# Reordering the first two stages of a retention and feed-forward kernel: two blocks of tokens per quarter of the weights, weight conversion ahead of a chunk that loads late

## The chip, the core and the metric

The kernel runs on one core of a Trainium2 (trn2) chip. The metric is the device time of one execution in microseconds; the figure quoted for a kernel is the median of its executions. The engines are called as the profile calls them: PE is TensorE (matrix products, and transposes as products with an identity), PEld its weight load, DVE is VectorE, ACT is ScalarE, POOL is GpSimd, SP starts the transfers.

## The reference

```python
# q, k, v: (8, 8, 576, 64) float32
scores = scale * q @ k^T                    # per batch and head
ret    = (scores * Dmat[head]) @ v          # Dmat: causal mask with a decay
x      = ret.transpose(0, 2, 1, 3).reshape(4608, 512)
a, b   = x @ w1, x @ w2                     # w1, w2: (512, 1024) float64
h      = (a * b) @ w3                       # w3: (1024, 1024) float64
out    = (h @ w_out).astype(float32)        # w_out: (1024, 512) float64
```

The weights arrive as float64, that is as pairs of 32-bit words, and the chip itself turns them into float32. They are cut into 40 blocks of 128 x 512: 16 for w1 and w2 (four in each quarter), 8 for w_out, 16 for w3.

## The kernel before

The eight batches are taken in four pairs. A pair is five chunks of the sequence (`NC`) for the attention, and three blocks of 192 tokens per batch (`NB`) for the products with w1 and w2. Those are done by quarters of the weights (`NQ` = 4), each by Strassen's scheme. A *unit* is one block of tokens times one quarter: seven products of eight matrix instructions. It needs three things: the quarter converted, the sums S1 to S4 of the weights (DVE), and the sums T of the tokens (POOL).

```python
def scale(g, nm):                       # decay into q or v of chunk g
    nc.gpsimd.tensor_tensor(out=t[:sz], in0=t[:sz], in1=..., op=ALU.mult)

def front(g):                           # 16 transposes of k and q, copied out by ACT
    ...
    nc.scalar.copy(dst[:, b, :, :sz], tp[:, :, :sz])

def score(g):                           # scores, then the mask product on DVE
    ...
    nc.vector.tensor_mul(pm[:sz, b, j, :, :sz], sc[j][:sz, :, :sz], mask...)

# state(g): running k^T v, 32 instructions; pv(g): the attention's output, copied by ACT into xT

def begin_block():                      # three DVE steps and two exponent operations on ACT
    vec.tensor_scalar(out=e, in0=hi, ...); yield
    vec.tensor_scalar(out=m, in0=hi, ...); yield
    vec.scalar_tensor_tensor(m.bitcast(F32), in0=lo.bitcast(U32), ...)
    nc.scalar.activation(e, e, relu, bias=lim[:, 0:1], scale=-1.0)
    nc.scalar.activation(e, e, relu, bias=lim[:, 1:2], scale=-2.0 ** 23)
    yield

def end_block():                        # two more DVE steps, then the next load
    vec.scalar_tensor_tensor(e, in0=hi, ..., in1=e, ...); yield
    vec.scalar_tensor_tensor(out, in0=m, ..., in1=e, ...)      # into wA
    load_block()
    if key[0] == "w12" and key[2:] == (1, 1):
        strassen_weights(key[1])        # S1, S2, S3, S4: four DVE sums into wS and wA
    yield

# convert(n): n of these steps. convert_up_to(n): steps until block n is converted.

def strassen_tokens(i, n):              # four subtractions on POOL, three T buffers
    T = [ffn.tile([P, 2, TB], F32, tag="T", name="T", bufs=4) for _ in range(3)]
    ...

def up(i, n, fp, conv=0):               # the unit: block n of pair i, quarter fp
    convert_up_to(4 * (fp + 1))
    if ("B", i, n) not in live:
        strassen_tokens(i, n)
    ...
    c = ffn.tile([P, 4, 2, TB], F32, tag="c", name="c")        # two buffers
    p1 = product(None, "A11", "B11")
    nc.scalar.copy(c[:, 0], p1)
    plus(product(None, "S2", "T2"), 1, 0)   # plus: DVE sum, then convert(conv)
    ...                                     # five more products: four DVE sums, one ACT copy
    nc.vector.tensor_mul(ab[:, 4 * fp:4 * fp + 4, :], c[:, :, 0, :], c[:, :, 1, :])
    convert(conv)

# ---- main program, first part ----
for g in range(NC):
    if g + 1 < NC:
        if g + 2 < NC:
            load(g + 2, "kq")
        scale(g + 1, "q"); front(g + 1); scale(g + 1, "v")
    pv(g)
    if g + 2 < NC:
        load(g + 2, "v")
    if g == 1:
        strassen_tokens(0, 0)
    if g + 1 < NC:
        state(g + 1)
        if g == 1:
            convert_up_to(KD)           # KD = 4: quarter 0
        else:
            convert(10)
        score(g + 1)
    if 0 < g < NC - 1:
        up(0, 0, g - 1, conv=1)         # block 0 alone, one quarter per chunk
...
todo = [(0, n, fp) for n in range(NB) for fp in range(NQ)][NC - 2:]
while multiplied < KF:                  # w3 @ w_out, row by row, with units between
    if todo:
        up(*todo.pop(0), conv=1)
    if multiplied < turned[0]:
        w3_mm(multiplied); multiplied += 1
    if turned[0] < KF and (not todo or ...):
        convert_up_to(...); w3_tr(turned[0]); turned[0] += 1
    convert(10 if not todo else 3)
...
# ---- pairs 1 to 3: chunks, with the units and output products of the pair before between them ----
for g in range(NC, G):
    ...
    pv(g)
    ...
    if g + 2 < G:
        scale(g + 2, "q")
    work(n // 2)
```

Each engine's queue is filled in program order, so a step of the conversion stands behind whatever the program put on DVE or ACT before it. And the loads of weights and of chunks share SP's queue, in program order too.

## Time and profile before

| | before |
|---|---|
| median time | 973.8 us (973.47 to 974.25) |
| span of the profiled execution | 974.7 us |
| PE busy / idle | 911.0 / 63.7 us |

The prediction below says in which stretches PE idles, and shows the lines. A row of the costliest groups gives, after the count, busy time, the mean in ns of one instruction, and after the second bar the idle time just before those instructions with its main releaser. One row carries the question, that of the products whose weights are the sums S on tokens T:

```profile
L410 PE MATMUL up<-T,wS 128*128 128x192 f32 x768 | 148.8, 339 | 26.6 <-DVE wS L134 21.2
```

Of 63.7 us of idleness, 26.6 stand before this group, 21.2 of them put down to DVE's sums. Line numbers of the two kernels differ by one or two (L410 becomes L412, L134 becomes L133, L385 becomes L387); "up" is the unit's product. A *cold spell* is a stretch behind a wait in which PE's groups take longer, up to twice as long (2.90 us in place of 1.46 for eight instructions), at a low granted clock.

### The profile page before, as it was taken

To read this page: it belongs to the slowest core of one execution; us is meant where nothing else is said; L and a number is where in the kernel's file an instruction comes from. 1 tells how busy PE (TensorE), PEld (TensorE's weight loads), DVE (VectorE), ACT (ScalarE), POOL (GpSimd) and SP (SyncE) were. 2 spreads that over 40 slices of the span, in tenths; PEclk is the share of its full clock that TensorE was granted. 3 is DMA by queue.
4 is the path that set the end of the run, shared out by engine and by line. 5 is a ranking of instruction groups with operands and counts; after the bars stand their busy time and mean duration, and the time that the engine had idled before them with its cause. 6 is when DMAs were issued, how large, how long until landed. Compare 5 with 4: busy or idle time off the path is not lost.

```text
span 974.7 us, 14094 instructions
## 1 busy us (share of the span) xinstructions
PE 911.0 (93%) x6085; PEld 722.6 (74%) x6085; DVE 349.3 (36%) x597; ACT 202.5 (21%) x373; POOL 126.0 (13%) x95
## 2 busy tenths in 40 slices
PE   5467779999999998999999999999999999999998
PEld 4466669976445666995995985986977968869593
DVE  1496778956500111341331330331331412313030
ACT  3323334323412222011111112011111111010100
POOL 3320010100030232220110121111110100101000
PEclk9777879999999999899999999999999999999999
DMA  9965323212342656030303302216010000010101
GB/s 164 185 120 129 87 87 106 91 64 91 71 75 57 121 108 140 2 66 22 77 1 66 66 2 54 44 29 131 4 34 22 1 11 22 1 33 1 32 1 33
DMA packets 126382, 59.69 MB, mean 61 GB/s; under 512 B 114536, under 2 KB 114536, under 8 KB 126320
## 3 DMA queue, kind: packets, MB, share of 16 engines
q1 hardware_dynamic: 124992, 58.73, 27.0%
q8 instruction: 48, 0.79, 0.3%
q10 hardware_dynamic: 1328, 0.06, 0.1%
q14 instruction: 14, 0.11, 0.0%
HBM read 49.34 MB, written 9.44 MB: 60 GB/s over the span
## 4 chain that ended last, share of the span: by engine, by line
PE 87%; DVE 6%; DMA 3%; ACT 1%; SPq 1%; issue 1%; POOL 0%; ACTq 0%; POOLq 0%; DVEq 0%
PE up L410 45%; PE po L441 25%; PE ps L369 5%; PE xps L237 3%; PE tp L173 3%; PE sc L188 3%; PE xps L230 2%; PE st L209 1%; DMA ld_q<-in_q_dram 1%; DVE e L317 1%; DVE m L303 1%; DVE wA L326 1%; DMA raw<-in_moe_w_dram 1%; DMA ld_v<-in_v_dram 1%; SPq L149 1%
## 5 line engine op out<-in xcount | busy, mean ns | idle before, releaser
L415 DVE TENSOR_TENSOR c<-up,c 128x384 f32<-128x384 f32 x240 | 133.6, 557 | 373.4 <-PE up L410 371.2
L441 PE MATMUL po<-w3o,ab 128*128 128x512 f32 x576 | 251.0, 593 | 0.0
L410 PE MATMUL up<-xT,wA 128*128 128x192 f32 x1152 | 219.4, 334 | 7.3 <-DVE wA L326 7.3
L410 PEld LDWEIGHTS up<-xT,wA 128*128 128x128 f32 x1152 | 196.5, 195 | 12.7 <-DVE wA L326 8.5
L441 PEld LDWEIGHTS po<-w3o,ab 128*128 128x128 f32 x576 | 108.2, 190 | 129.2 <-issue 128.4
L410 PE MATMUL up<-T,wS 128*128 128x192 f32 x768 | 148.8, 339 | 26.6 <-DVE wS L134 21.2
L410 PEld LDWEIGHTS up<-T,wS 128*128 128x128 f32 x768 | 134.7, 199 | 28.2 <-issue 22.5
L191 DVE TENSOR_TENSOR pm<-sc,mask 128x512 f32<-128x512 f32 (+1 forms) x80 | 45.4, 628 | 196.4 <-PE sc L188 196.4
L428 ACT COPY c<-up 128x384 f32<-128x384 f32 x48 | 23.0, 479 | 259.3 <-PE up L410 259.2
L410 PE MATMUL up<-xT,wS 128*128 128x192 f32 x384 | 70.5, 327 | 0.5 <-DVE c L415 0.5
L444 ACT COPY ot<-po 128x512 f32<-128x512 f32 x36 | 21.1, 586 | 238.6 <-PE po L441 238.6
L410 PE MATMUL up<-T,wA 128*128 128x192 f32 x384 | 70.2, 326 | 0.0
L385 POOL TENSOR_TENSOR T<-xT,T 128x384 f32<-128x384 f32 x24 | 24.6, 1025 | 346.9 <-PE up L410 346.7
L157 POOL TENSOR_TENSOR ld_q<-ld_q,gq 128x1024 f32<-128x1024 f32 (+1 forms) x20 | 38.5, 1923 | 221.8 <-DMA ld_q<-in_q_dram 221.8
L410 PEld LDWEIGHTS up<-xT,wS 128*128 128x128 f32 x384 | 63.6, 190 | 1.1 <-DVE c L415 1.1
L410 PEld LDWEIGHTS up<-T,wA 128*128 128x128 f32 x384 | 63.7, 190 | 0.0
L157 POOL TENSOR_TENSOR ld_v<-ld_v,gk 128x1024 f32<-128x1024 f32 (+1 forms) x20 | 38.3, 1915 | 169.6 <-DMA ld_v<-in_v_dram 162.9
L369 PE MATMUL ps<-wo,w3T 128*128 128x512 f32 x128 | 56.9, 597 | 1.9 <-ACT w3T L363 1.9
L434 DVE TENSOR_TENSOR ab<-c 128x768 f32<-128x768 f32 x48 | 46.2, 962 | 3.8
L369 PEld LDWEIGHTS ps<-wo,w3T 128*128 128x128 f32 x128 | 23.8, 190 | 30.1 <-issue 26.8
L306 ACT ACTIVATE e<-e,lim 128x512 int32<-128x512 int32 x40 | 28.9, 723 | 66.3 <-DVE e L296 66.2
L188 PE MATMUL sc<-qT,kT 64*128 64x128 f32 (+1 forms) x640 | 38.6, 271 | 0.0
(48 smaller groups left out, 568.0 us busy)
## 6 DMA issues: line engine op xcount, KB each, us to landing
ld_k<-in_k_dram SPq DMA_DIRECT2D x16, 512.0 KB, 6.4
ld_q<-in_q_dram SPq DMA_DIRECT2D x16, 512.0 KB, 7.5
ld_v<-in_v_dram SPq DMA_DIRECT2D x16, 512.0 KB, 4.5
raw<-in_moe_w_dram SPq DMA_DIRECT2D x32, 256.0 KB, 5.7
raw<-in_moe_w_dram SPq DMA_DIRECT2D x16, 512.0 KB, 3.3
out_dram<-ot SPq DMA_DIRECT2D x24, 256.0 KB, 2.0
raw<-in_moe_w_out_dram SPq DMA_DIRECT2D x8, 512.0 KB, 3.5
out_dram<-ot SPq DMA_DIRECT2D x24, 128.0 KB, 2.4
```

The costliest lines, as they stand in the source:

```text
L157: nc.gpsimd.tensor_tensor(out=t[:sz], in0=t[:sz], in1=gam[:sz, c].rearrange("p b h -> p (b h)").unsqueeze(2).to_broadcast([sz, 2 * H, D]), ...
L173: nc.tensor.transpose(tp[:, p, :sz], src[:sz, h:h + 2, :].rearrange("p a d -> p (a d)"), ident[:sz, :sz])
L188: nc.tensor.matmul(sc[j][:sz, p, :sz], kT[hs, b, p, :sz], qT[hs, b, p, :sz], start=True, stop=True)
L191: nc.vector.tensor_mul(pm[:sz, b, j, :, :sz], sc[j][:sz, :, :sz], mask[:sz, :sz].unsqueeze(1).to_broadcast([sz, NP, sz]))
L237: nc.tensor.matmul(banks[r][heads[half], b, n, :sz], vs[:sz, b * H + 2 * p + j, :], pm[:sz, b, j, p, :sz], start=(c == 0 and m == 0), stop ...
L306: nc.scalar.activation(e, e, relu, bias=lim[:, 0:1], scale=-1.0)
L369: nc.tensor.matmul(ps, live["w3T", ft][:, g, :], live["wo"][:, g, :], start=(g == 0), stop=(g == KF - 1))
L385: nc.gpsimd.tensor_tensor(out=out, in0=in0, in1=in1, op=ALU.subtract)
L410: nc.tensor.matmul(ps[:, w, :], a[:, w, r, :], b[:, r, :], start=(new and w == r == 0), stop=(w == r == 1), skip_group_check=True)
L415: nc.vector.tensor_add(c[:, to], ps, c[:, sb])
L434: nc.vector.tensor_mul(ab[:, 4 * fp:4 * fp + 4, :], c[:, :, 0, :], c[:, :, 1, :])
L441: nc.tensor.matmul(po, ab[:, f, t * P:(t + 1) * P], live["w3o"][:, f, :], start=(f == 0), stop=(f == KF - 1))
```

## The change

The intent is to have fewer units at the start that wait for a quarter of the weights. A quarter, once converted, serves block 0 and block 1 instead of block 0 alone, so PE has work while DVE converts the next one. The conversion of quarter 0 is put ahead of chunk 2's front, whose loads come late. Beside this, the product of a w3 row is split around the next row's transposes, the token sums of pair 1 are made well ahead, with six T buffers for four, and c has one buffer for two.

```diff
-        c = ffn.tile([P, 4, 2, TB], F32, tag="c", name="c")
+        c = ffn.tile([P, 4, 2, TB], F32, tag="c", name="c", bufs=1)
-        T = [ffn.tile([P, 2, TB], F32, tag="T", name="T", bufs=4) for _ in range(3)]
+        T = [ffn.tile([P, 2, TB], F32, tag="T", name="T", bufs=6) for _ in range(3)]
...
-    for g in range(NC):
-        ...                      # the loop shown above
+    ...
+    score(1)
+    convert_up_to(4)
+    load(3, "kq")
+    scale(2, "q")
+    pv(1)
+    load(3, "v")
+    strassen_tokens(0, 0)
+    scale(2, "v")
+    front(2)
+    state(2)
+    score(2)
+    up(0, 0, 0, conv=1)
+    convert(4)
+    load(4, "kq")
+    scale(3, "q")
+    pv(2)
+    load(4, "v")
+    scale(3, "v")
+    front(3)
+    state(3)
+    score(3)
+    up(0, 0, 1, conv=1)
+    pv(3)
+    strassen_tokens(0, 1)
+    up(0, 1, 0, conv=1)
+    scale(4, "q")
+    scale(4, "v")
+    up(0, 1, 1, conv=1)
+    front(4)
+    score(4)
+    up(0, 0, 2, conv=1)
+    pv(4)
...
-    todo = [(0, n, fp) for n in range(NB) for fp in range(NQ)][NC - 2:]
+    todo = [(0, 1, 2), (0, 0, 3), (0, 1, 3)] + [(0, 2, fp) for fp in range(NQ)]
     while multiplied < KF:
         if todo:
             up(*todo.pop(0), conv=1)
-        if multiplied < turned[0]:
-            w3_mm(multiplied)
-            multiplied += 1
+            convert(3)
+        ft = multiplied
+        begun_ft = ft < turned[0]
+        if begun_ft:
+            w3_mm(ft, 0)                  # first half of the product
         if turned[0] < KF and (...):
             ...
             w3_tr(turned[0])
             turned[0] += 1
-        convert(10 if not todo else 3)
+        if begun_ft:
+            w3_mm(ft, 1)                  # second half
+            multiplied += 1
+        if not todo:
+            convert(10)
...
         pv(g)
+        if g == NC + 1:
+            strassen_tokens(1, 0)
```

Left out: the third ab buffer's pool is opened only after the attention of pair 0, `load(2, "kq")` stands ahead of chunk 0, and a unit no longer forms the next block's token sums where they already exist.

More of the change, by code (lines that the diff above doesn't have):

```diff
@@ L79 @@
     raw = weights_part.enter_context(tc.tile_pool(name="raw", bufs=2, side="right"))
-    ab3 = weights_part.enter_context(tc.tile_pool(name="ab3", bufs=1, side="right"))
     pools = {}
@@ L105 @@
     gq = const.tile([P, NC, 2, H], F32, tag="gq", name="gq")
-    dq = ffn.tile([P, 4, 2, TB], F32, tag="c", name="dq").rearrange("p a b s -> p (a b s)")[:H, :S]
+    dq = ffn.tile([P, 4, 2, TB], F32, tag="c", name="dq", bufs=1).rearrange("p a b s -> p (a b s)")[:H, :S]
     nc.scalar.dma_start(dq, decay_q)
@@ L364, in w3_tr, with w3_mm @@
         live["w3T", ft] = t
-    def w3_mm(ft):
-        ps = acc.tile([P, DM], F32, tag="acc", name="ps")
-        for g in range(KF):
+    def w3_mm(ft, part):
+        if part == 0:
+            live["w3ps"] = acc.tile([P, DM], F32, tag="acc", name="ps")
+        ps = live["w3ps"]
+        for g in range(part * NP, part * NP + NP):
             nc.tensor.matmul(ps, live["w3T", ft][:, g, :], live["wo"][:, g, :],
                              start=(g == 0), stop=(g == KF - 1))
-        nc.scalar.copy(live["w3o"][:, ft, :], ps)
+        if part == 1:
+            nc.scalar.copy(live["w3o"][:, ft, :], ps)
     every = [(i, n) for i in range(NB2) for n in range(NB)]
@@ L399, in up @@
         if fp == 0:
-            live["ab", i, n] = (ab3 if m == 2 else ffn).tile([P, 2 * KF, TB], F32, tag="ab", name="ab")
+            live["ab", i, n] = (pools["ab3"] if m == 2 else ffn).tile([P, 2 * KF, TB], F32, tag="ab", name="ab")
         ab = live["ab", i, n]
@@ L430, in up @@
         plus(p5, 1, 1)
-        if fp == NQ - 1 and m + 1 < len(every) and has_x(*every[m + 1]):
+        if fp == NQ - 1 and m + 1 < len(every) and has_x(*every[m + 1]) and ("B", *every[m + 1]) not in live:
             strassen_tokens(*every[m + 1])
@@ L466 @@
         load_block()
+    load(2, "kq")
     scale(0, "q")
@@ L471 @@
     score(0)
-    for g in range(NC):
-        if g + 1 < NC:
-            if g + 2 < NC:
-                load(g + 2, "kq")
-            scale(g + 1, "q")
-            front(g + 1)
-            scale(g + 1, "v")
-        pv(g)
-        if g + 2 < NC:
-            load(g + 2, "v")
-        if g == 1:
-            strassen_tokens(0, 0)
-        if g + 1 < NC:
-            state(g + 1)
-            if g == 1:
-                convert_up_to(KD)
-            else:
-                convert(10)
-            score(g + 1)
-        if 0 < g < NC - 1:
-            up(0, 0, g - 1, conv=1)
+    scale(1, "q")
+    front(1)
+    scale(1, "v")
+    pv(0)
+    load(2, "v")
+    state(1)
+    convert(10)
[31 more added lines that the diff above has]
+    pv(4)
     att_part.close()
+    pools["ab3"] = weights_part.enter_context(tc.tile_pool(name="ab3", bufs=1, side="right", reuse_waits="tile"))
     pools["wst"] = w3_part.enter_context(tc.tile_pool(name="wst", bufs=2, side="right", reuse_waits="tile"))
@@ L511 @@
             turned[0] += 1
-        convert(10 if not todo else 3)
+        if begun_ft:
+            w3_mm(ft, 1)
+            multiplied += 1
+        if not todo:
+            convert(10)
     w3_part.close()
```

## The prediction

> **What bounds the kernel now.** I read the page's busy line and slices first, then the engine windows, then TensorE's waits, then the timelines of TensorE and VectorE up to 180 us.
>
> ```profile
> PE 911.0 (93%) x6085; PEld 722.6 (74%) x6085; DVE 349.3 (36%) x597; ACT 202.5 (21%) x373; POOL 126.0 (13%) x95
> PE   5467779999999998999999999999999999999998
> PEclk9777879999999999899999999999999999999999
> ```
>
> TensorE (PE) is busy 911.0 of 974.7 us, so 63.7 us are all that removed waits can give directly. Nearly all lie in the first six slices (about 146 us), where the granted clock is low too. One more clock dip, a single 8, stands in the sixteenth slice. The windows give sizes:
>
> ```profile
> 24.00:143.00 119.00, 78.35 (x689) 72.90 (x690) 85.83 (x138) 39.11 (x64) 21.94 (x15) 0.78 0.55 121
> 143.00:284.00 141.00, 137.70 (x643) 104.15 (x642) 90.39 (x163) 50.34 (x84) 11.12 (x7) 1.00 0.33 88
> 384.00:400.00 16.00, 10.62 (x50) 10.32 (x49) 1.89 (x4) 2.02 (x5) 8.56 (x7) 0.79 0.34 72
> ```
>
> The columns are length, then busy time of PE, PEld, DVE, ACT, POOL, then clock, DMA share, GB/s. From 24 to 143 us PE idles 119.0 - 78.35 = 40.7 us at clock 0.78; from 143 to 284 it idles 3.3 us, and from 384 to 400 it idles 5.4 us. The waits name the causes:
>
> ```profile
> PE up L410 <- DVE wS L134: 21.2, 4, 6.8
> PE up L410 <- DVE wA L326: 7.3, 4, 3.9
> PE up L410 <- POOL T L385: 5.4, 1, 5.4
> ```
>
> The four large waits are one per quarter of w1 and w2: the unit (seven Strassen products) waits until VectorE (DVE) has converted the quarter's four 64-bit blocks and formed the sums S1 to S4. What makes that late at the start:
>
> ```profile
> 33.33 0.69 DVE L303 SCALAR_TENSOR_TENSOR m<-raw,m 128x512 f32<-128x512 uint32 x1
> 46.99 1.11 DVE L317 SCALAR_TENSOR_TENSOR e<-raw,e 128x512 int32<-128x512 int32 x1 [12.97 <-ACT e L307]
> 49.54 2.01 DVE L296 TENSOR_SCALAR e<-raw 128x512 int32<-128x512 int32 x1
> 57.24 2.90 PE L410 MATMUL up<-T,wS 128*128 128x192 f32 x8 [6.76 <-DVE wS L134]
> 66.55 1.46 PE L410 MATMUL up<-xT,wS 128*128 128x192 f32 x8
> ```
>
> DVE sits idle 12.97 us for an exponent operation on ScalarE (ACT), which has the copies of chunk 2's transposes ahead of it, whose k and q land at 33.65 and 36.06 us.
>
> **What the Trainium skill says.** "TensorE: Matmul & The Clock Gate", Part 1 (Architectural detail), calls the queues of ScalarE and VectorE strict FIFO. The trace agrees: ACT's two exponent operations run at 46.87 us, right behind the copies, though their input was ready at 33.3. The same page, Part 1 (What's actually happening), says that the clock is halved after an idle window of about 3.4 us, and restored after as much activity. The trace agrees: eight matmul records take 2.90 us after a wait, against 1.46. A warm unit is 7 x 1.3 = 9.1 us, whereas the rest after each wait took 10.6, 10.9, 9.8 and 10.7 us in place of 7.8: each wait costs 2.0 to 3.1 us more. "SBUF — State Buffer", Who interferes with whom, says that VectorE (two SBUF inputs or a 2-port mode) and GpSimd (POOL) lock each other out of a shared port pair for a whole instruction. The trace agrees: the L296 operation above took 2.01 us beside a POOL scaling, 0.43 elsewhere.
>
> **The change part by part.** No arithmetic is added or removed, so PE's work stays; what moves is the start.
>
> (1) *Conversion ahead of chunk 2.* The conversions of quarter 0 now come before chunk 2's front on DVE and ACT. DVE resumes at 30.5 us (end of the mask product of chunk 1). From the timeline a block costs 2.85 us (124.96 to 127.81), five steps of 0.57; the sums cost 2.6, and S2, which the second product wants, is there after 1.4. Undisturbed quarter 0 ends at about 41; I allow 46.5, since POOL's seven microseconds of scaling and token sums lie beside it. Now the tokens set the start: chunk 1's transposed copy 38.5, four POOL sums 43, scaling of v 45.2, state and scores 48.3. So unit (block 0, quarter 0) runs from 48.3, cold for a while (+2): 59.4. Before: 67.85.
>
> (2) *Quarter 1.* Chunk 2's product and chunk 3's front, state and scores (7.7 us, as at 67.85 to 75.54 before): 67.1. In DVE's order the mask product of chunk 3 (2.4 us, starting 66.1) precedes two blocks (5.7) and S1, S2 (1.4): 75.6. PE waits some 7 us in all; unit 7.8 + 3.1 cold: 86.5. Before: 94.84.
>
> (3) *Second block of tokens.* Chunk 3's product (2.9), its copy (1.0), then POOL's sums (second one at 93.2) hold the second product for about 1 us; then two whole units on quarters already there: 101.0 and 110.1. Meanwhile DVE does 18 of the steps of quarter 2. Chunk 4's front and scores end at 114.2; mask product, last two steps, S1, S2: 118.5. The wait is some 3 us, half of a cold spell (+0.7): 127.0. Product of chunk 4: 129.9. Unit (1, 2): 139.0.
>
> (4) *Quarter 3 is still late.* DVE has only interleaved steps in these two units. After PE's end: last sum, multiply and two steps (2.6), three steps of the explicit conversion (2.0), five more (2.85), S1 and S2 (1.4): 147.9, a wait of some 8 us in two parts; 7.8 + 2.9 cold: 158.6. Unit (1, 3): 167.7, and four units of block 2: 204.1.
>
> (5) *Comparison.* Before, unit (0, 3) ended at 142.89 with eight units left: 142.89 + 72.8 + 1.4 (waits of 0.48 and 0.90) = 217.1 for the same work. Gain here: **13.0 us**. For w3, halves of a product now surround the next transpose and hide its copy: 1.9 us of waits on ACT go, but w3's conversion is no further ahead, so about 2 us of wait appear at the first two rows. Gain 0: I take 12.6 in all.
>
> (6) *Token sums of pair 1.* They now follow chunk 6's product. In the trace their wait is 5.38 us at 391.39, and the next five groups of eight records are 3.0 us slow (2.72 + 2.56 + 1.62 against 3 x 1.3). The sums take 4 us on a POOL that is free most of that stage. Gain **8.4 us**. Six T buffers in place of four permit it.
>
> (7) *One c buffer.* The next unit's first copy waits for the multiply: about 0.3 us after where it would be, behind PE, which has seven PSUM buffers. I take zero.
>
> Sum 12.6 + 8.4 = 21.0: 952.8. I put 954.5, since a schedule worked out by hand leaves out more delays than gains.
>
> **The rivals.** *DVE is the bound of the whole start, and waits only move:* it is busy 85.83 of 119 us, and block 2's units no longer lie between the w3 rows. For it: steps (2) and (4) keep two waits of 7 to 8 us in my own schedule. Against it: 13 us of DVE's idleness goes and two units fill waits. If conversion slips further into w3, the first part shrinks to about 5 us: 960. *POOL's lock or late loads:* chunk 3 now loads behind three weight blocks, with DMA at 0.96 share from 25 to 50 us; if its q lands after 61 us, or POOL's sums push quarter 0 past 48.3, each microsecond adds one: 956 to 960. *The better case:* the remaining waits are shorter and stay warm (two cold spells of 3 us avoided): 948.
>
> **Range and chances.** The 2% line is 973.8 x 0.98 = 954.3, on top of my estimate. The 8.4 us are sure as such things go; the 12.6 could be 6 to 18. So 954.5 with 949 to 961; slower by 2% would take a hang-up for which I see no sign: 0.01. Faster by over 2%: 0.47; within: 0.52.
>
> **What will show it.** Right: DVE's 12.97 us wait on ACT is gone; the first unit starts at 47 to 50 us; four units run in blocks 0 and 1 before quarter 2 is wanted; a wait of 6 to 9 us stays at quarters 1 and 3 and about 3 at quarter 2; the wait on POOL's T at pair 1 is gone with its cold spell; end of the w3 products near 271 us (283.4 before); PE's idle time falls from 63.7 to about 52 us, and the rest of the gain, some 10 us, is busy time that runs on the full clock (three cold spells of 2.0 to 3.1 us fewer or shorter in the first stage, one at pair 1, a warmer chunk 2). Wrong: a wait on loads of chunk 3 or 4, PE waiting for c or a PSUM buffer, or w3's conversion holding PE after 204 us.

## The result, and the profile after

The result is correct. Its median is 960.62 us (959.19 to 963.53, four runs) against 973.82. A ratio here is the mean time of one kernel's fast runs over the mean of the other's fast runs of the same rounds, so it is not quite the ratio of the medians; it is 0.9868, with a 95% interval of 0.9841 to 0.9895. The change is faster by 1.3%, which is inside 2%. The prediction of 954.5 was 6.1 us too low; its range (949 to 961) held the time, near its upper end. In the later batch the same kernel took 959.20 us (958.68 to 959.94), ratio 0.9852. Below, an experiment's gain or loss is given against both figures where they were not of one batch. The first four runs fall in two groups, 959.2 twice, and 962.01 and 963.53, and their median lies between these; 959.20 is the cleaner figure to compare with.

The page of the changed kernel, its busy line and two of its slices:

```profile
PE 908.7 (95%) x6085; PEld 718.8 (75%) x6085; DVE 350.9 (37%) x597; ACT 202.9 (21%) x373; POOL 127.0 (13%) x95
PE   5488898989999999999999999999999999999998
PEclk9697997989999999999999999999999999999999
```

PE works 2.3 us less and idles 960.3 - 908.7 = 51.6 us, 12.1 less. The dips near 390 us (PE's in the sixteenth slice, the clock's in the seventeenth, not the sixteenth as the prediction has it) are gone. The first six slices (now 144 us) read 5 4 8 8 8 9 where they read 5 4 6 7 7 7. The windows, with the columns explained in the prediction, for the start, for the stage up to the end of block 2, and for the w3 products:

```profile
24.00:143.00 119.00, 93.56 (x808) 87.13 (x804) 85.13 (x135) 36.90 (x64) 21.27 (x14) 0.87 0.53 112
143.00:206.00 63.00, 57.29 (x331) 56.53 (x332) 53.19 (x97) 22.12 (x36) 4.81 (x4) 0.92 0.29 92
206.00:274.00 68.00, 64.63 (x194) 31.99 (x193) 39.44 (x70) 30.30 (x49) 7.56 (x4) 0.95 0.47 112
```

From 24 to 143 us PE idles 25.4 us where it idled 40.7. A part of that only moved: quarter 3 is now wanted after 143 us, and from there to 206 us PE idles 5.7 us, against 1.4 before. DVE is busy 85.13 us there, as before (85.83): it did not become busier, PE did. PE's waits (sum, number, longest):

```profile
PE st L208 <- POOL ld_v L156: 10.4, 3, 6.4
PE up L412 <- DVE wS L133: 8.8, 3, 3.0
PE up L412 <- DVE wA L325: 7.1, 2, 3.6
PE ps L370 <- ACT w3T L362: 2.5, 1, 2.5
PE up L412 <- POOL T L387: 0.6, 1, 0.6
```

The waits on DVE's sums fell from 21.2 to 8.8 us, and the wait of 5.4 us on POOL's T is gone. On POOL's scaling of v PE now waits 10.4 us, with one wait of 6.4, where one of 3.7 stood before, and a wait of 2.5 us in the w3 products is new. PE's timeline (start, duration, operation, count, and in brackets the idle time before it with the releaser) shows each at its place:

```profile
45.90 1.97 PE L208 MATMUL st<-ld_v,ld_k 128*64 128x64 f32 x32 [6.42 <-POOL ld_v L156]
...
51.74 1.46 PE L412 MATMUL up<-T,wS 128*128 128x192 f32 x8
...
76.95 2.90 PE L412 MATMUL up<-T,wS 128*128 128x192 f32 x8 [3.03 <-DVE wS L133]
...
150.35 2.90 PE L412 MATMUL up<-T,wS 128*128 128x192 f32 x8 [2.75 <-DVE wS L133]
...
210.77 6.40 PE L370 MATMUL ps<-wo,w3T 128*128 128x512 f32 x8 [2.46 <-ACT w3T L362]
...
336.41 1.09 PE L172 MATMUL tp<-ident,ld_q 128*128 128x128 f32 x8 [2.46 <-POOL ld_q L156]
```

The second product of the first unit starts at 51.74, against 57.24 before, and does not wait. Those of quarters 1 and 3 still wait for DVE. At 336.41, in pair 1, is a wait that the kernel before had not. The work up to the end of block 2, that is all twelve units of pair 0, ends at 206.17 us; the prediction works out 217.1 for the same work before.

### The profile page after: what moved, and what is told of

It is laid out like the page before. It is cut to its first block, busy times and chain, and to the rows that moved or that the text cites. A ratio compares the mean times of both kernels' runs of the same rounds, so it can differ in the third digit from the quotient of the medians.

```text
span 960.3 us, 14136 instructions
## 1 busy us (share of the span) xinstructions
PE 908.7 (95%) x6085; PEld 718.8 (75%) x6085; DVE 350.9 (37%) x597; ACT 202.9 (21%) x373; POOL 127.0 (13%) x95
## 4 chain that ended last, share of the span: by engine, by line
PE 90%; DVE 4%; POOL 1%; ACT 1%; DMA 1%; SPq 1%; issue 1%; ACTq 0%; DVEq 0%
PE up L412 45%; PE po L443 26%; PE ps L370 6%; PE xps L236 3%; PE sc L187 3%; PE tp L172 3%; PE xps L229 2%; PE st L208 1%; DMA raw<-in_moe_w_dram 1%; POOL T L387 1%; DVE pm L190 1%; SPq L148 1%; PE tp L360 1%; DVE wA L325 1%; DVE e L316 1%
## 5 line engine op out<-in xcount | busy, mean ns | idle before, releaser
L412 PE MATMUL up<-xT,wA 128*128 128x192 f32 x1152 | 217.1, 332 | 7.6 <-DVE wA L325 7.1
L412 PE MATMUL up<-T,wS 128*128 128x192 f32 x768 | 144.5, 332 | 9.4 <-DVE wS L133 8.8
L412 PEld LDWEIGHTS up<-T,wS 128*128 128x128 f32 x768 | 130.5, 194 | 10.9 <-issue 10.0
L430 ACT COPY c<-up 128x384 f32<-128x384 f32 x48 | 23.0, 479 | 245.4 <-PE up L412 239.9
L370 PE MATMUL ps<-wo,w3T 128*128 128x512 f32 x128 | 59.1, 616 | 2.5 <-ACT w3T L362 2.5
L236 PE MATMUL xps<-pm,ld_v 128*64 128x128 f32 (+1 forms) x640 | 38.4, 272 | 4.1 <-DVE pm L190 4.1
L423 ACT COPY c<-up 128x384 f32<-128x384 f32 x48 | 22.9, 477 | 88.9 <-DVE ab L436 57.0
```

Source lines behind the costliest of these rows:

```text
L236: nc.tensor.matmul(banks[r][heads[half], b, n, :sz], vs[:sz, b * H + 2 * p + j, :], pm[:sz, b, j, p, :sz], start=(c == 0 and m == 0), stop ...
L370: nc.tensor.matmul(ps, live["w3T", ft][:, g, :], live["wo"][:, g, :], start=(g == 0), stop=(g == KF - 1))
L412: nc.tensor.matmul(ps[:, w, :], a[:, w, r, :], b[:, r, :], start=(new and w == r == 0), stop=(w == r == 1), skip_group_check=True)
```

## The experiments

Twelve kernels were run, five rounds each, every batch beside runs of the kernel before on the same chip (medians 973.87, 974.02 and 973.89 us). All gave correct results. Unless stated, an edit is against the changed kernel.

| run | median, us | ratio to before (95%) |
|---|---|---|
| a1_tokens_late | 963.86 | 0.9909 (0.9889 to 0.9929) |
| a2_tokens_after_scale | 956.58 | 0.9821 (0.9808 to 0.9833) |
| a3_w3_copy_first | 958.34 | 0.9843 (0.9826 to 0.9860) |
| a4_convert_behind | 962.78 | 0.9885 (0.9872 to 0.9898) |
| b1_one_block | 965.27 | 0.9910 (0.9897 to 0.9924) |
| b2_old_start | 965.74 | 0.9917 (0.9903 to 0.9930) |
| b3_v_scale_first | 955.56 | 0.9820 (0.9803 to 0.9837) |
| b4_before_one_c | 974.27 | 1.0001 (0.9988 to 1.0015) |
| c0_after_again | 959.20 | 0.9852 (0.9838 to 0.9865) |
| c1_three_queues | 952.30 | 0.9776 (0.9762 to 0.9789) |
| c2_mask_later | 940.17 | 0.9654 (0.9641 to 0.9668) |
| c3_more_steps | 936.71 | 0.9622 (0.9608 to 0.9637) |

The theory to test was: the gain comes from three separate places (the order at the start, two blocks per quarter, pair 1's token sums), and what is short of the prediction sits in three waits that *the change's own order in a queue* makes: at 45.90, 210.77 and 336.41 us. The main rivals were that DVE is the bound of the start and waits only move, and that the order of the loads, not that of the conversion, counts.

### Pair 1: a1_tokens_late and a2_tokens_after_scale

a1 takes the early token sums out; a2 keeps them, but behind the scaling of the next q in POOL's queue.

```diff
 # a1 and a2
         pv(g)
-        if g == NC + 1:
-            strassen_tokens(1, 0)
 # a2 only
             scale(g + 2, "q")
+        if g == NC + 1:
+            strassen_tokens(1, 0)
         work(n // 2)
```

> The changed kernel with one part undone: the token sums of pair 1 are formed when its first unit is reached, as before. The prediction valued this part at 8.4 us (5.4 us wait on GpSimd's T and 3.0 us of cold clock). The trace of the changed kernel shows a new wait of 2.46 us at the transposes of a later chunk, because the four sums stand ahead of a q scaling in GpSimd's queue. Theory 'moved wait': this run is slower than the changed kernel by 5.4 to 6.5 us (8.4 less 2.46), about 966.5; the 5.4 us wait on T comes back and the 2.46 us wait goes. Rival 'whole gain': 8 us or more slower, 969. Rival 'hidden': under 2 us.

> The changed kernel with the token sums of pair 1 one step later on GpSimd, behind the scaling of the next q instead of ahead of it. Theory 'moved wait': the 2.46 us wait of the transposes on the q scaling goes, nothing replaces it, so about 958.2, 2.5 us faster than the changed kernel (960.6). Rival: the q comes late from its load anyway and the wait only changes its name: no difference.

a1 lost 3.2 us against the first runs of the changed kernel and 4.7 against the later ones. PE's timeline of a1 has the old wait back:

```profile
379.21 2.93 PE L412 MATMUL up<-T,wS 128*128 128x192 f32 x8 [4.89 <-POOL T L387]
```

It is 4.89 us here (5.38 in the kernel before), and the slow records behind it cost 1.8, while the 2.46 us at 336 us are gone: 4.89 + 1.8 - 2.46 = 4.2, which fits the loss. The expectation was right in kind and somewhat too large. Two of its six runs took 968 us; why is open.

a2 gained 2.6 us against the later runs and 4.0 against the first. In its timeline the same transposes start without a wait:

```profile
331.03 1.04 PE L172 MATMUL tp<-ident,ld_q 128*128 128x128 f32 x8
```

So the wait at 336.41 was made by the place of four POOL subtractions in POOL's queue, in front of a scaling that PE needed sooner. It is removed by moving two lines, and against the later runs the gain is about the wait's length.

### The w3 products: a3_w3_copy_first

The copies of a transposed w3 row are on ACT, behind exponent operations of the conversion. a3 puts fewer conversion steps ahead of them after the last unit.

```diff
             up(*todo.pop(0), conv=1)
-            convert(3)
+            convert(3 if todo else 1)
```

> The changed kernel with two conversion steps fewer after the last unit of block 2, so that ScalarE's queue has the copy of the first transposed w3 row ahead of the next block's exponent operations. In the changed kernel the first w3 product waited 2.46 us for that copy and then ran 8 records in 6.40 us in place of about 3.6. Theory 'queue order on ScalarE': wait falls to about 0.6 us, no cold spell, some of it given back as a wait for the second row's conversion (1 to 2 us): 3 us faster than the changed kernel, about 957.5. Rival 'VectorE is the bound there': the wait only moves to the second row's transposes, gain under 1 us.

The time was 958.34 us: 2.3 better than the first runs, 0.9 better than the later ones. PE's timeline of a3:

```profile
207.07 3.60 PE L370 MATMUL ps<-wo,w3T 128*128 128x512 f32 x8
...
213.06 0.63 PE L360 MATMUL tp<-ident,w 128*128 128x128 f32 x4 [1.95 <-DVE w L325]
```

The wait on ACT is gone and most of it comes back as 1.95 us on DVE's conversion of the next row. At the first rows of w3, then, the wait only changes its name, as the rival said; the gain of 0.9 us against the later runs is inside the spread of a3's own (956.26 to 960.08). What the wait on ACT costs depends on the clock behind it. In the repetition c0 the same wait of the changed kernel was followed by a full clock, but the other wait of this length, that on q in pair 1, was not:

```profile
209.70 3.70 PE L370 MATMUL ps<-wo,w3T 128*128 128x512 f32 x8 [2.47 <-ACT w3T L362]
...
333.57 8.73 PE L443 MATMUL po<-w3o,ab 128*128 128x512 f32 x16
```

The eight records of the first line took 6.40 us in the first profile; the sixteen of the second, which follow the transposes that waited 2.46 us, took 7.03 there. So each of the two profiled executions lost time behind one of the two waits: the first (962.01 us) 2.7 us in w3, c0's (959.94 us) 1.7 in pair 1. With the same wait on ACT, a1, a2, a4 and b2 show 3.70 us, and b3, whose profiled execution is the slowest of its four (959.31 us), shows 6.39. Whether the spread between runs comes from here is not shown, since only the profiled executions have a trace; a3's runs, which lack the wait on ACT, spread by 3.8 us all the same.

### The order at the start: a4_convert_behind and b2_old_start

a4 puts chunk 2's front ahead of the conversion of quarter 0, as it was, but keeps chunk 3's loads behind quarter 0's weights. It also puts chunk 2's v scaling ahead of the token sums, as it was; b3, below, makes that one swap alone. b2 also restores the order of the loads and lets chunk 3's scalings on POOL run as early as they did. Both keep two blocks per quarter.

```diff
 # a4
     score(1)
-    convert_up_to(4)
-    load(3, "kq")
     scale(2, "q")
+    front(2)
+    scale(2, "v")
     pv(1)
-    load(3, "v")
     strassen_tokens(0, 0)
-    scale(2, "v")
-    front(2)
     state(2)
+    convert_up_to(4)
+    load(3, "kq")
+    load(3, "v")
     score(2)
 # b2: as a4, but
+    load(3, "kq")          # ahead of scale(2, "q"); load(3, "v") after pv(1)
+    scale(3, "q")          # both ahead of up(0, 0, 0)
+    scale(3, "v")
```

> The changed kernel with conversion of quarter 0 put back behind chunk 2's front (loads in the changed order). Theory 'one chain': VectorE's wait of about 13 us on ScalarE returns, the first unit's second product starts near 57 in place of 51.7 us, and all later steps shift with it, since each quarter is converted between units: 6 to 8 us slower than the changed kernel, about 967.5. Rival 'VectorE has slack later': the later waits for quarters 1 to 3 shrink by as much and the end moves by under 3 us.

> As a4 (conversion of quarter 0 behind chunk 2's front), and chunk 3's loads also back ahead of the weight blocks, as before. Theory 'load order counts through GpSimd': chunk 3's q and v land early again, GpSimd scales them while VectorE converts quarter 0, both hold each other up, and the first unit's second product starts near 57 us (53.8 in a4, 51.7 in the changed kernel): about 3 us slower than a4, 965.5. Rival: load order does not count, same as a4, 962.8.

a4 lost 2.2 to 3.6 us, b2 5.1 to 6.5: a4 far less than its theory said, b2 as expected. PE's timeline of a4, second products of quarters 0 and 1, and DVE's at quarter 0:

```profile
53.84 2.90 PE L412 MATMUL up<-T,wS 128*128 128x192 f32 x8 [3.48 <-DVE wS L133]
...
81.63 2.90 PE L412 MATMUL up<-T,wS 128*128 128x192 f32 x8 [2.74 <-DVE wS L133]
```

```profile
46.88 1.10 DVE L316 SCALAR_TENSOR_TENSOR e<-raw,e 128x512 int32<-128x512 int32 x1 [12.55 <-ACT e L306]
```

and of b2, quarter 0, with DVE's timeline of b2 behind it:

```profile
56.87 2.90 PE L412 MATMUL up<-T,wS 128*128 128x192 f32 x8 [6.76 <-DVE wS L133]
```

```profile
46.63 1.10 DVE L316 SCALAR_TENSOR_TENSOR e<-raw,e 128x512 int32<-128x512 int32 x1 [12.50 <-ACT e L306]
...
49.17 2.01 DVE L295 TENSOR_SCALAR e<-raw 128x512 int32<-128x512 int32 x1
51.10 2.12 DVE L299 TENSOR_SCALAR m<-raw 128x512 int32<-128x512 int32 x1
```

b2 has the old start back: 56.87 against 57.24 before, and DVE idle for 12.50 us, against 12.97, behind ACT's copies. In a4, with the loads left as changed, DVE's wait is back too, 12.55 us. So the mechanism that the prediction named, exponent operations stuck in ACT's queue, is confirmed by undoing it. Against the changed kernel the delay is only 2.1 us at quarter 0 (53.84 - 51.74), and 3.6 to 4.7 at quarter 1. This is no measure of the conversion's order, since a4 takes the v scaling out of PE's way at the same time. The fair partner is b3, which has the v scaling where a4 has it and the conversion ahead of the front: there the second product starts at 48.40, 5.4 us before a4's, and the median is 955.56, 7.2 us below a4's. That is the size that the theory named, 6 to 8 us. (In a4 the attention's output of chunk 1, and so the token sums, come later too, but its first unit waits for DVE, 1.77 and 3.48 us, and not for tokens.) The two were run in different batches, whose medians of the kernel before differ by 0.15 us.

The load order comes on top, and it acts through POOL. In b2 chunk 3's q and v are scaled at 48.55 and 50.86 us, for 2.35 and 2.08 us, and the two DVE steps beside them take 2.01 and 2.12 us in place of 0.43. In a4 the scaling of q comes at 58.41, when quarter 0 is done; POOL had stood idle for 9.57 us, waiting for that load, so the load's place decides and not POOL's queue. The 3 us between a4 and b2 are this.

### One block per quarter again: b1_one_block

```diff
     up(0, 0, 1, conv=1)
-    pv(3)
-    strassen_tokens(0, 1)
-    up(0, 1, 0, conv=1)
     scale(4, "q")
-    scale(4, "v")
-    up(0, 1, 1, conv=1)
     front(4)
+    scale(4, "v")
+    pv(3)
+    convert(10)
     score(4)
     ...
-    todo = [(0, 1, 2), (0, 0, 3), (0, 1, 3)] + [(0, 2, fp) for fp in range(NQ)]
+    todo = [(0, n, fp) for n in range(NB) for fp in range(NQ)][NC - 2:]
```

> The changed kernel with the order of units undone: quarters 2 and 3 are used by block 0 as soon as they exist, and block 1 follows whole, as before; conversion ahead of chunk 2, the load order and pair 1 stay changed. Worked out from the kernel before, where 15.4 us lay between the end of the second unit and the second product of the third and 12.3 us between the end of the third and the second product of the fourth: fourth unit's end near 136, eight units more 209, against 206.2 in the changed kernel. Theory 'the order of units is worth little, since the conversion steps then run in the waits without interleaving': 2 to 4 us slower, about 963.5. Rival 'two blocks per quarter is the main part of the gain': 8 us or more slower, 969.

It lost 4.7 to 6.1 us, between its theory and its rival. Not all is due to the order of the units. Moving chunk 4 up made POOL scale its q and v while DVE converted quarter 1. DVE's timeline of b1 has the sign of it, and PE's has the effect:

```profile
71.14 2.12 DVE L299 TENSOR_SCALAR m<-raw 128x512 int32<-128x512 int32 x1
...
74.63 2.27 DVE L325 SCALAR_TENSOR_TENSOR wA<-m,e 128x512 f32<-128x512 f32 x1
```

```profile
81.35 2.90 PE L412 MATMUL up<-T,wS 128*128 128x192 f32 x8 [2.74 <-DVE wS L133]
```

These two steps lie beside POOL's scalings at 70.88 and 74.08. The second product of quarter 1 starts at 81.35, 3.3 to 4.4 us later than in the two profiles of the changed kernel, before any unit of block 1 is due. The fourth unit ends at 140.89; with eight more of 9.1 us the twelve units would end at 213.7 (in the run, w3 rows lie between them). That is 7.5 us later than in the first profile of the changed kernel and 8.6 later than in c0 (205.10), so 3 to 5 us are left for the order of the units. The headline idea, taken alone, is worth less than the rearrangements at the start together. Of the whole time still less is left, 0.3 to 2.8 us (4.7 less 4.4, 6.1 less 3.3), since b1's first w3 rows lie between units and do not wait for ACT. This split is a subtraction with side effects in it, so the size is an estimate.

### The v scaling: b3_v_scale_first

```diff
     load(3, "v")
-    strassen_tokens(0, 0)
     scale(2, "v")
+    strassen_tokens(0, 0)
     front(2)
```

> The changed kernel with two GpSimd jobs swapped: the scaling of chunk 2's v ahead of the four token sums of block 0. In the changed kernel TensorE waits 6.42 us for that scaling before chunk 2's state product. Theory 'GpSimd's queue sets the first unit': state and scores end near 43.5, the first unit's second product starts when S2 is there, near 47 (51.7 before), and the rest shifts: 4 us faster than the changed kernel, about 956.5. Rival 'VectorE sets it': S2 or the mask product is pushed back by the same GpSimd jobs, and the gain is under 1 us.

The time was 955.56 us, 3.6 to 5.1 better, as expected. The profiled execution is the slowest of the four. PE's timeline of b3:

```profile
41.96 1.98 PE L208 MATMUL st<-ld_v,ld_k 128*64 128x64 f32 x32 [1.06 <-POOL ld_v L156]
...
48.40 1.46 PE L412 MATMUL up<-T,wS 128*128 128x192 f32 x8
```

The wait fell from 6.42 to 1.06 us and the second product starts 3.3 us earlier. DVE's last sum of quarter 0 ended no later for it (46.7 us against 47.6), so at this place POOL's order was the bound, and neither DVE nor the loads.

### One c buffer: b4_before_one_c

The kernel before, with only this part of the change.

```diff
-        c = ffn.tile([P, 4, 2, TB], F32, tag="c", name="c")
+        c = ffn.tile([P, 4, 2, TB], F32, tag="c", name="c", bufs=1)
```

(The tile that shares the tag is set to one buffer too.)

> The kernel before with one c buffer in place of two, and nothing else. In the changed kernel ScalarE's first copy of a unit waits 57 us in all for VectorE's multiply. Theory 'that wait is off the path, since seven PSUM buffers decouple TensorE': 973.8, within 1 us. Rival 'it costs 0.2 us or more per unit': 48 units, 10 us slower.

The time was 974.27 us, ratio 1.0001. The waits of ACT show how much waiting that is:

```profile
ACT c L421 <- DVE ab L434: 53.9, 22, 2.7
```

ACT now waits 53.9 us for DVE's multiply, and the time does not move: the waiting is off the path that sets the end. The prediction's zero is confirmed. Built with two c buffers, the changed kernel does not fit, by the builder's message: 16 KB per partition are wanted for the w3 product where 15.19 are left.

### The gains together: c0_after_again, c1_three_queues, c2_mask_later, c3_more_steps

c0 is the changed kernel. c1 is a2, a3 and b3 together. c2 adds to c1 that DVE converts a whole quarter ahead of a mask product that is not urgent. c3 adds to c2 more conversion steps, and chunk 4's front ahead of unit (1, 1).

```diff
 # c2, against c1
     state(3)
+    convert_up_to(8)
     score(3)
     ...
     front(4)
+    convert_up_to(12)
     score(4)
 # c3, against c2
     strassen_tokens(0, 1)
+    convert(4)
     up(0, 1, 0, conv=1)
     ...
-    up(0, 1, 1, conv=1)
     front(4)
+    convert(3)
+    up(0, 1, 1, conv=1)
     convert_up_to(12)
     score(4)
     up(0, 0, 2, conv=1)
+    convert(5)
     pv(4)
```

> The changed kernel itself, once more, on the chip of the next three. 959 to 963.5 as in its first four runs. Theory 'clock phase': its runs fall in two groups about 2.8 us apart, since the wait at the first w3 product (2.46 us) sometimes brings a cold clock and sometimes not.

> The changed kernel with the three queue orders of a2, a3 and b3 together: pair 1's token sums behind the next q scaling, the w3 copy ahead of the exponents, v's scaling ahead of block 0's token sums. If the three are independent the gains add: 2.5 + 2.5 + 4.5 = 9.5 us faster than the changed kernel, about 951. Rival 'VectorE is the bound of the start and takes them back': 955.

> c1, and on VectorE the rest of quarter 1 ahead of chunk 3's mask product, the rest of quarter 2 ahead of chunk 4's. VectorE idled 2.79 us for the scores of chunk 3 while quarter 1 was unfinished, and both mask products (2.4 us) are wanted only after the following unit. Theory 'the order on VectorE sets these two waits': S2 of quarter 1 comes 5 us earlier and of quarter 2 3 us earlier, one cold spell of 2.9 us goes: 9 to 11 us faster than c1, about 941. Rival 'VectorE's total work is the bound': the wait reappears at quarter 3, gain under 3 us.

> c2, and conversion steps put where VectorE idled in order: 4 after block 1's token sums, 3 after chunk 4's front, 5 after the unit (0, 2); chunk 4's front one unit earlier. Theory 'quarter 3 is late only because steps are bound to units': the wait of about 6.3 us at quarter 3 and its cold spell of 2.9 us shrink by 3 to 8 us: about 936. Rival: ScalarE's queue puts exponents ahead of copies that TensorE wants, or VectorE falls behind TensorE: no gain over c2.

c0's four runs are one group, so the two groups of its theory did not come again. c1 took 952.30 us, 6.9 better than c0; the single gains against the later figure are 2.6, 0.9 and 3.6, so they add up (the 9.5 expected counted more for each). c2 took 940.17, another 12.1 (9 to 11 expected). PE's timeline of c2 at quarters 1, 2 and 3:

```profile
68.94 2.02 PE L412 MATMUL up<-T,wS 128*128 128x192 f32 x8 [2.15 <-DVE wS L133]
...
107.19 1.46 PE L412 MATMUL up<-T,wS 128*128 128x192 f32 x8
...
136.02 2.90 PE L412 MATMUL up<-T,wS 128*128 128x192 f32 x8 [2.74 <-DVE wS L133]
```

Quarter 1 waits 2.15 us where it waited 3.56 and 3.03 in two parts (3.55 and 2.75 in c1), quarter 2 not at all where it waited 3.05 (in c1 too), and quarter 3, for which nothing was changed, as before. The changed kernel's remaining waits at quarters 1 and 2 were thus not a lack of DVE time. They were DVE's queue. DVE's timeline of the changed kernel has the line:

```profile
67.29 2.48 DVE L190 TENSOR_TENSOR pm<-sc,mask 128x512 f32<-128x512 f32 x4 [2.79 <-PE sc L187]
```

A mask product, whose result is wanted only after the unit, stood in front of two blocks of quarter 1. DVE idled 2.79 us for its scores and then took 2.48 us for it, 5.3 us in all, while PE waited 6.6 us for these blocks.

c3 took 936.71 us, another 3.5, at the lower end of the 3 to 8 expected. The window of c3, then two lines of its PE timeline:

```profile
24.00:143.00 119.00, 102.71 (x868) 97.09 (x861) 106.43 (x168) 43.69 (x74) 27.05 (x18) 0.91 0.55 129
```

```profile
136.70 2.76 PE L412 MATMUL up<-xT,wS 128*128 128x192 f32 x8 [1.91 <-DVE c L417]
...
180.93 0.77 PE L360 MATMUL tp<-ident,w 128*128 128x128 f32 x4 [3.90 <-DVE w L325]
```

The wait at quarter 3 is gone, too. Now DVE is busy 106.43 of 119 us (85.13 in the changed kernel), PE waits 1.91 us until a DVE sum has read the PSUM tile that the next product adds to, and the w3 rows, reached earlier, wait 3.90 us for DVE's conversion. Here the rival "DVE is the bound of the start" begins to be true. c3 is the best version: 3.8% below the kernel before, and 22.5 us below c0.

## Why the prediction was right or wrong

The trace gained 974.7 - 960.3 = 14.4 us where the sum said 21.0, so 6.6 us are missing. In this execution they lie in three terms: 2.1 in the first stage, 1.9 in w3, 2.6 in pair 1. In c0's trace the gain is 974.7 - 958.2 = 16.5 us: 12.0 by the end of block 2 (205.10), 12.4 by the end of w3 (270.87), and 4.1 behind it, where the cold spell stood that time. So the shares of w3 and pair 1 depend on which of their two waits of 2.5 us brings the low clock.

**Step (1), conversion ahead of chunk 2: right in mechanism and, by two errors that cancel, in size.** DVE's wait on ACT is gone, and b2 brings it back. The unit ended at 59.64 (predicted 59.4). It started at 50.34, not 48.3, since the scaling ended 0.7 us late and state and scores ran at the low clock, in 4.4 us and not 3.1; but then it ran warm, where I had added 2 us. The step treats POOL's order of token sums before the v scaling as given and counts it in full, but never asks whether it was needed; b3 shows 3.6 to 5.1 us in that swap. It is also incomplete in its cause: beside the conversion's order (some 7 us, b3 against a4) the load order, through POOL's lock, is worth 3 (a4 against b2). The step's ground, the strict queue on ACT, is right, but one reading in it is a pair of operations off: the operations that DVE waited for ran at 45.48 and 46.24 us and ended at 46.96, where DVE goes on; their input was ready at 27.85. Those at 46.87 belong to the next block.

**Steps (2) to (4): right in kind, each a little short.** The ends were 87.95 for 86.5, 101.8 and 110.9 for 101.0 and 110.1, 129.4 for 127.0, 141.6 for 139.0, 160.4 for 158.6. The waits stay at the places and near the sizes named: 6.6 us at quarter 1 (some 7 predicted), 3.05 at quarter 2 (some 3), 6.3 at quarter 3 (some 8). Step (2) even lists the mask product ahead of the two blocks; it took that order as fixed, where c2 shows that it was what most of the waits at quarters 1 and 2 came from. The term that failed most is the cold spell of quarter 2, which I put at 0.7 us, half of one: from the second product at 119.77 to the end are 9.65 us in place of 7.8, so it was 1.9, and the start itself was 1.3 late (118.5 predicted). Block 2 ended at 206.17 for 204.1, so the first part of the gain was 10.9 and not 13.0.

**Step (5), w3: the term was mis-sized in this execution.** "Gain 0" was put down (2 us of waits going, 2 us coming), with 0.4 taken off (13.0 to 12.6). The products behind w3 start at 274.64 us, 8.6 earlier than before (283.23); of the 10.9 gained by then, 2.3 were lost again, 1.9 more than allowed. The waits in w3 are 0.90 us, which the kernel before had among its units, and 2.46, which is new; the second brought, in this execution, a record group of 6.40 us in place of some 3.7. In c0's execution this did not happen, and w3 cost nothing. a3 shows that the wait on ACT can be moved off, but comes back at DVE.

**Step (6), pair 1: one half of the queue was overlooked.** The wait of 5.38 us and its 3.0 us at the low clock went, as predicted: 8.4. But "a POOL that is free most of that stage" was not free at the one place that counted: the sums stood in front of a scaling, and PE waited 2.46 us for that. Measured gain: 14.4 less the 8.6 gained by the end of w3, or 5.8 us, and 4.1 in c0. This is the largest of the three terms, and a2 recovers it by two lines: its span behind w3 (271.88 to 954.8) is 8.6 us shorter than before (283.23 to 974.7), close to the 8.4 predicted. (The three groups that the step lists are what was slow, not five.)

**Step (7): zero, confirmed by b4.**

**The idle time** was predicted at about 52 us and measured at 51.6. But then "the rest of the gain, some 10 us, is busy time" failed: PE's busy time fell only by 2.3 us, since the waits that stayed or came were long enough to bring cold spells with them. The schedule itself did not hold these 10 us: its low-clock terms in the first stage fall from 10.8 (2.8 + 3.1 + 2.0 + 2.9) to 8.7 (2 + 3.1 + 0.7 + 2.9), which with the 3.0 of pair 1 makes 5.1.

**The rivals.** "DVE is the bound and waits only move" is refuted for this version (c2 gains 12.1 us by DVE's order alone) and begins to hold in c3. "POOL's lock or late loads" was the nearest: no load held the units of the changed kernel, but POOL's queue did, at 45.90, and it held transposes at 336.41. My range was right because I had put it wide above the estimate for delays that a schedule by hand leaves out; I had not named these delays. It was also luck: the median lies 0.4 us inside, and two of the four runs lie above 961. The chances, 0.47 for over 2% and 0.52 for within, leaned to the right side by little. Of the signs, the start of the first unit (47 to 50) was missed by 0.3 us and the end of w3 (near 271) by 3.6, though c0 has 270.87.

One part was not isolated: the split of the w3 product into halves was never run alone, so its worth is open.

## What to carry to other kernels

When work is moved ahead on a helper engine, look for what it now stands in front of: three of this change's own waits were a not yet urgent operation ahead of an urgent one in POOL's or ACT's queue, and another order of program lines took 19 us off (c0 to c2) at equal work. Before taking the helper engine for the bound because its steps end the waits, compare its busy time in that stage with the stage: DVE was busy 85 of 119 us, and stayed useful up to 106. When a change is undone to measure it, look for what else the edit moves: a4 seemed to halve the conversion's worth until it was set against b3. And count a wait of 2 us or more at its length plus up to 3 us of low clock behind it, which need not come in every execution.

## What the Trainium skill lacked or had wrong

- "SBUF — State Buffer", Who interferes with whom: the lock between DVE and POOL agrees with the runs. What the page lacks is the cost seen from a chain of short instructions. Beside POOL's scalings of 2.1 to 2.35 us each, DVE steps that otherwise take 0.42 to 0.69 us took 2.0 to 2.3, one DVE step to one POOL operation (b1, b2). Two scalings that nobody was waiting for delayed a quarter by 3 us (b2 against a4).
- "TensorE: Matmul & The Clock Gate", Part 1 (What's actually happening): the page's idle window of about 3.4 us is no safe threshold to plan with. In c3 a wait of 2.16 us was followed by two groups of 2.36 and 2.37 us in place of 1.46, and in the changed kernel a wait of 2.46 us (with one of 0.90 shortly before) was followed by 6.40 us for eight records in one execution and by 3.70 in another. The page says that the window runs freely and that the count of slow records varies between runs; these runs agree with that, and show it in the middle of a kernel, with a spread of 2.7 us in one place.
- "TensorE: Matmul & The Clock Gate", Part 1 (Architectural detail): strict FIFO queues on ACT and DVE agree with the runs. No page that I read draws the consequence that bound this kernel: DVE stood still for 12.97 us since an exponent operation whose input was ready stood behind copies whose own input was late.
